# First chunk laid out as two batches by two tokens per partition, W2 loaded by SyncE and cast on chip, and all steps in a new order

## The chip, the cores and the metric

The kernel runs on one core of one Trainium2 chip. The core has five engines that work side by side, each through its own list of instructions, in order: TensorE (PE in the profile; PEld are its weight loads), VectorE (DVE), ScalarE (ACT), GpSimd (POOL) and SyncE (SP), which here only issues DMAs. The metric is the device time of one execution in microseconds; the median of several runs is given. A profile is taken of one execution, and its times count from the first instruction of that execution.

## The reference

The computation has two parts. The first is a linear recurrence over 768 tokens, for 4 batches and 8 heads of width 48:

```
state = 0                                     # per batch and head, 48 x 48
for t in range(768):
    y[t]  = r[t] @ (state + outer(u * k[t], v[t]))
    state = w[:, None] * state + outer(k[t], v[t])
```

`w` (the decay) and `u` have one value per head and channel. The 8 heads of a token, put side by side, make one row of 384 numbers, and the 3072 rows (4 batches by 768 tokens) are the input x of the second part, a feed-forward layer with a squared relu:

```
h   = maximum(x @ w_in, 0)        # 384 -> 2048
out = (h * h) @ w_out             # 2048 -> 384
```

All inputs and the output are 32-bit floats. The kernel multiplies in bf16 and sums in 32 bits.

## The kernel before

**Units.** The tokens are cut into 6 chunks of 128, and a unit is one chunk of one batch: unit i is chunk i // 4 of batch i % 4, 24 in all. Inside a chunk the recurrence is turned into matrix products. k is scaled with powers of the decay that fall with the token's place, r with powers that rise (steps `kh` and `rh`, L336 and L339, into one tile `rk`). `T` (L363) transposes `rk` on TensorE, eight 128 x 128 transposes a unit, and `Tc` copies the result out of PSUM; from unit 7 on a transposing DMA does both (`XB`, L369). `A` (L376) multiplies k by r per head, `Bm` (L384) masks the product to earlier tokens, `Y` (L394) multiplies that with v (in bf16, made by `vb`) and, from the second chunk on, adds r times the state (L392). The term with `u` is computed apart: `P0`, `P1`, `du` and `dv` make the products and sums r*k*u and multiply them into v; `xs` (L411) adds them to Y and gives x. `U` (L403) makes the chunk's contribution to the state, and `S0`, `ts`, `S` keep the state per batch. `X` (L429) and `xTc`, or the DMA `xX`, transpose x.

**Feed-forward.** Units are joined in groups, the first two alone and the others in pairs. `F1` (L445) computes x @ w_in for a group in slices into a PSUM bank, `re` (L453, L455) takes the relu, `sq` (L460 to L464) the square; for a group of two there are 8 slices of 2 x 128 hidden columns. `F2` (L472) sums the product with w_out over the 16 blocks of hidden columns, in quarters of four matmuls per unit; `os` copies the sum out of PSUM, `out` stores it. The last unit is split in two column halves (`F2c`, L486).

**Weights.** w_in is cut into 8 slices `W1[s]`. Seven are loaded in 32 bits by SyncE's queue (`lW`, L324) and cast to bf16 by an engine (`cW`, L260 on ACT or L262 on POOL). One, and all of w_out (`W2`, four slices), are loaded by GpSimd's queue (`W`, L333), which casts on the way.

**Dummies.** `Z` (L498, L500) are matmuls of the identity with itself; their results are not used. They stand at the start, where TensorE has nothing else.

**Order.** There is no scheduler at run time. `ORDER`, a list of steps written out by hand or by a planner ahead of time, sets the list of every engine: `kh.1:D/0` is step kh of unit 1 on DVE into buffer 0. A is ACT, D is DVE, G is GpSimd, P is TensorE, S is SyncE. An engine waits at an instruction until its operands are there and its buffer is free, and everything behind it waits too; that holds for the loads in SyncE's list as well. Buffers per kind are given by `POOLS`; before the change the eight PSUM banks are split into 4 for attention, 2 for F1 and 2 for F2. A DMA that is issued when earlier ones are under way can have to wait at its issuing engine for one of them to end.

Of the kernel before, what the change touches and what calls it, by code (L numbers as in the profile page):

```python
# [19 lines left out]
ORDER = """  # L20
w:A Z.8.4:P Z.8.5:P Z.8.4:P Z.8.5:P Z.8.4:P Z.8.5:P ld.k.1:S/0 ld.r.1:S/0 u:S shw:D shu:D tab:A ld.r.3:S/1 logw:A
Z.6.4:P P0.1:G/0 ld.r.0:S/2 ld.k.0:S/1 Wk:A/0 Wt:A/1 kh.1:D/0 ld.v.1:S/0 rh.3:D/1 ld.k.3:S/2 P1.1:G rh.0:D/2 Z.8.5:P
P0.0:G/1 rh.1:D T.1:P/0 Z.8.4:P Z.5.5:P kh.0:D Tc.1:A/0 Z.6.4:P T.0:P/1 ld.r.2:S/3 Tc.0:A/1 A.0:P/2/3 vb.1:A/0 P0.3:G/2
du.1:D/0 dv.1:G ld.v.0:S/1 A.1:P/0/1 Z.8.5:P Z.8.4:P P1.0:D ld.k.2:S/3 kh.3:D du.0:D/1 Bm.0.1:D/0 P0.2:G/3 P1.3:D
Bm.1.1:D/1 rh.2:D/3 kh.2:D lW.0.1:S/0 T.3:P/3 Tc.3:A/2 lW.0.6:S/1 Bm.0.0:D/2 ld.v.2:S/2 WtS:A cW.0.1:A P1.2:G lW.0.7:S/2
T.2:P/1 Z.8.5:P Z.8.4:P Z.6.5:P Bm.1.0:D/3 lW.0.0:S/3 cW.0.7:G ld.v.3:S/3 Tc.2:A/3 du.2:D/2 Y.1:P/3 vb.0:A/1 xs.1:D/0
A.2:P/2/0 cW.0.6:A vb.2:D/2 dv.0:G X.1:P/1 Y.0:P/3 lW.0.5:S/0 xTc.1:A/0 Bm.2.0:D/4 Bm.2.1:D/5 lW.0.4:S/2 dv.2:G
A.3:P/1/2 wc:S Z.4.4:P Bm.3.0:D/3 cW.0.0:A W.0.2:G xs.0:D/1 du.3:D/3 vb.3:G/3 lW.0.3:S/1 U.2:P/0 F1.1.3:P/1 Bm.3.1:D/1
Y.2:P/1 xs.2:D/2 re.1.3:A/0 X.0:P/3 F1.1.0:P/0 xTc.0:A/1 F1.0.0:P/1 dv.3:G Y.3:P/2 xs.3:D/3 X.2:P/1 ld.r.4:S/4 U.0:P/3
re.1.0:A/1 xTc.2:A/0 W.1.0:G F1.0.3:P/0 cW.0.5:G W.1.1:G X.3:P/2 cW.0.4:A xTc.3:A sq.1.0:A0/0 re.0.0:D/2 ld.k.4:S/4  # L30
ld.r.5:S/5 U.3:P/1 F1.0.2:P/1 WLcol:A re.0.3:D/3 ld.k.5:S/5 re.0.2:D/4 F1.1.2:P/0 sq.0.0:A0/1 W.1.2:G W.1.3:G ld.k.7:S/6
# [530 lines left out]
```

## Time and profile before

| what | value |
|---|---|
| median of 3 runs | 174.29 us (173.12 to 174.57) |
| span of the profiled execution | 172.5 us (the page gives no other time of it) |
| PE, PEld busy | 161.6 us, 121.2 us |
| DVE, ACT, POOL busy | 130.3, 111.1, 80.8 us |
| first F1 on PE | 19.11 us |
| first F1 of units 4 and 5 | 47.72 us |
| last matmuls (F2c) | 166.51 to 169.31 us |
| granted TensorE clock | 1.00 in all stretches |
| DMA | 105588 packets, 98008 of them under 512 B; 29.13 MB |

A row of a timeline gives start, length, engine, line, operation, output and inputs, and the count of instructions merged into it; in brackets stands the idle time ahead of it and what ended that. A row of the groups ends with the total busy time, the mean of one in nanoseconds, and the idle time ahead. A row of the stretches gives for each engine the busy time and the number of instructions, then granted clock, mean busy share of the 16 DMA engines and GB/s moved. In the chain of waits a row is start, length, and what the end of the program was waiting for at that time; SPq is SyncE's queue.

### The profile page before, as it was taken

How to read it: one execution, taken by the hardware profiler on the slowest of the kernel's cores; microseconds unless marked ns; L12 is line 12 of the kernel's file. 1: busy time of each engine (PE TensorE's matmuls, PEld its weight loads, DVE VectorE, ACT ScalarE, POOL GpSimd, SP SyncE). 2: the span in 40 equal slices, each digit the busy share in tenths (PEclk: the TensorE clock that was granted, in tenths of full speed). 3: DMA queues.
4: the chain of work that ended last, by engine and by line, in shares of the span. 5: the costliest groups of instructions: out<-in, count | busy, mean ns of one | idle time of the engine just before them, and what ended most of it. 6: DMA issues, size and time to landing. Idle time of an engine off the chain costs nothing.

```text
span 172.5 us, 4388 instructions
## 1 busy us (share of the span) xinstructions
PE 161.6 (94%) x1702; PEld 121.2 (70%) x1702; DVE 130.3 (76%) x259; ACT 111.1 (64%) x207; POOL 80.8 (47%) x98
## 2 busy tenths in 40 slices
PE   3976799979999999999999999999999999999992
PEld 1444788745788787787778768777778778777671
DVE  5768977739999896598789889888889894538300
ACT  2358787746379899858649647848858726532430
POOL 5644895108659298966937364047660204000000
PEclk9999999999999999999999999999999999999999
DMA  5999899989999989979999997998988330331022
GB/s 99 223 244 306 227 188 207 195 166 200 204 212 184 202 177 214 241 174 184 204 189 215 177 229 153 180 181 186 154 217 159 85 114 4 87 141 48 23 78 84
DMA packets 105588, 29.13 MB, mean 169 GB/s; under 512 B 98008, under 2 KB 105568, under 8 KB 105568
## 3 DMA queue, kind: packets, MB, share of 16 engines
q1 hardware_dynamic: 103672, 26.95, 72.7%
q0 software_dynamic: 1744, 1.77, 6.1%
q8 instruction: 13, 0.21, 0.5%
q10 hardware_dynamic: 152, 0.14, 0.2%
q14 instruction: 7, 0.06, 0.1%
HBM read 20.46 MB, written 4.72 MB: 146 GB/s over the span
## 4 chain that ended last, share of the span: by engine, by line
PE 76%; DMA 12%; SPq 8%; ACT 1%; POOL 1%; issue 1%; DVE 0%; POOLq 0%
PE bank L472 33%; PE bank L445 31%; DMA ldk<-in_k_dram 8%; SPq L320 6%; DMA wsa<-in_moe_w_in_dram 4%; PE bank L376 3%; PE bank L394 2%; PE bank L392 2%; SPq L324 2%; PE bank L403 2%; PE bank L486 2%; PE bank L429 1%; PE bank L363 1%; ACT W L260 1%; POOL urow L218 0%
## 5 line engine op out<-in xcount | busy, mean ns | idle before, releaser
L445 PE MATMUL bank<-xT,W 128*128 128x256 bf16 (+1 forms) x624 | 74.9, 264 | 0.2
L472 PE MATMUL bank<-W,hq 128*128 128x384 bf16 x368 | 69.3, 326 | 0.0
L453 ACT ACTIVATE hr<-bank 128x512 bf16<-128x512 f32 x75 | 44.4, 596 | 32.6 <-PE bank L445 27.1
L445 PEld LDWEIGHTS <-W 128*128 128x128 bf16 x624 | 55.2, 98 | 10.6 <-DVE hr L455 0.3
L472 PEld LDWEIGHTS <-hq 128*128 128x128 bf16 x368 | 34.8, 98 | 17.6
L460 ACT ACTIVATE hq<-hr 128x512 bf16<-128x512 bf16 x65 | 39.1, 628 | 0.3
L384 DVE TENSOR_TENSOR Bm<-bank,maskJT 128x512 bf16<-128x512 f32 x48 | 31.3, 684 | 7.3 <-PE bank L376 7.2
L346 POOL TENSOR_TENSOR P<-P,ub 128x384 f32<-128x384 f32 x15 | 16.1, 1079 | 13.9 <-DVE P L342 13.6
L455 DVE TENSOR_SCALAR hr<-bank 128x512 bf16<-128x512 f32 x21 | 14.3, 687 | 8.5 <-ACT hq L460 3.8
L342 POOL TENSOR_TENSOR P<-ldr,ldk 128x384 f32<-128x384 f32 x14 | 14.3, 1022 | 9.6 <-DMA ldk<-in_k_dram 6.0
L336 POOL TENSOR_TENSOR rk<-ldk,Wkhat 128x384 bf16<-128x384 f32 x10 | 10.0, 996 | 16.9 <-DMA ldk<-in_k_dram 16.9
L411 DVE TENSOR_TENSOR xs<-bank,dv 128x384 bf16<-128x384 f32 x24 | 13.0, 552 | 5.0 <-POOL dv L354 2.8
L354 POOL TENSOR_TENSOR dv<-ldv,du 128x384 f32<-128x384 f32 x18 | 14.8, 829 | 0.0
L349 DVE TENSOR_REDUCE du<-P 128x8 f32<-128x384 f32 x24 | 13.0, 544 | 0.6 <-POOL P L346 0.4
L260 ACT COPY rkT<-bank 128x1024 bf16<-128x1024 bf16 x7 | 7.1, 1012 | 9.1 <-PE bank L363 9.1
L339 POOL TENSOR_TENSOR rk<-ldr,Wt 128x384 bf16<-128x384 f32 x9 | 9.0, 996 | 7.0 <-DMA ldr<-in_r_dram 7.0
L260 ACT CAST vb<-ldv 128x384 bf16<-128x384 f32 x19 | 9.6, 511 | 4.1 <-DMA ldv<-in_v_dram 4.1
L498 PE MATMUL bank<-identity 128*128 128x512 bf16 x29 | 9.5, 471 | 2.7 <-POOL identity masks.py:199 2.7
L260 ACT COPY os<-bank 128x384 f32<-128x384 f32 (+1 forms) x15 | 7.0, 469 | 6.8 <-PE bank L472 4.5
L262 DVE COPY os<-bank 128x384 f32<-128x384 f32 (+1 forms) x10 | 5.2, 524 | 7.9 <-PE bank L486 4.3
L394 PE MATMUL bank<-vb,Bm 128*128 128x48 bf16 x192 | 11.0, 183 | 0.0
L464 DVE TENSOR_TENSOR hq<-hr 128x512 bf16<-128x512 bf16 x27 | 10.9, 432 | 0.0
(66 smaller groups left out, 166.5 us busy)
## 6 DMA issues: line engine op xcount, KB each, us to landing
ldk<-in_k_dram SPq DMA_DIRECT2D x24, 192.0 KB, 3.6
ldr<-in_r_dram SPq DMA_DIRECT2D x24, 192.0 KB, 3.6
ldv<-in_v_dram SPq DMA_DIRECT2D x24, 192.0 KB, 4.0
out_dram<-os SPq DMA_DIRECT2D x23, 192.0 KB, 2.3
wsa<-in_moe_w_in_dram SPq DMA_DIRECT2D x7, 384.0 KB, 5.6
W<-in_moe_w_out_dram POOLq DMA_DIRECT2D x4, 384.0 KB, 9.9
rkT<-rk SPq DMA_TRANSPOSE x17, 3.5
W<-in_moe_w_in_dram POOLq DMA_DIRECT2D x1, 192.0 KB, 6.3
```

The costliest lines, as they stand in the source:

```text
L260: e.copy(o, a)
L342: e.tensor_mul(P0b[slot[f"P{i}"]], loaded("r", i), loaded("k", i))
L346: e.tensor_mul(t, t, ub)
L349: e.tensor_reduce(dub[slot[f"dv{i}"]], P0b[slot[f"P{i}"]], axis=mybir.AxisListType.X, op=ALU.add)
L354: e.tensor_mul(dvb[slot[f"dv{i}"]], loaded("v", i), t)
L384: e.tensor_mul(Bmb[slot[f"Bm{i}{h}"]], heads(bank(f"bA{i}{h}"), 128), mask_b)
L394: e.matmul(y[:, hc, D * h : D * (h + 1)], m[h][:, hc, :], vb[:, 2 * hc + h, :], start=(c == 0), stop=True, skip_group_check=True,)
L445: e.matmul(hp[:, fi, :], W1[f // 2][:, c, 128 * (f % 2) : 128 * (f % 2 + 1)], xt[:, c, :], start=(c == 0), stop=(c == CCH - 1), skip_group ...
L453: e.activation(hr, hp, AF.Relu)
L455: e.tensor_scalar_max(hr, hp, 0.0)
L460: e.activation(hq, hr, AF.Square)
L472: e.matmul(bank(f"bO{i}", "bO")[:, 0:d_model], hqb[slot[f"hq{g},{f // m}"]][:, at : at + L], W2[q][:, f % 4, :], start=(f == 0), stop=(f = ...
```

## The change

Five things change.

1. **Layout of the first chunk.** Units 0 to 3 are no longer one batch each. Two batches share a tile: partitions 0 to 63 hold batch 2p, 64 to 127 batch 2p + 1, and each partition holds two neighbouring tokens. Unit 2p holds the even tokens of both batches, unit 2p + 1 the odd ones. A load then takes runs of 384 B instead of 192 B, and each of r, k, v comes for two units in two DMAs of 64 partitions, one per batch (`ldp`), six of them on SyncE's queue and six on ScalarE's. The scaling tables, masks and outputs follow: two tables each for k and r, a mask per parity, and two stores of 64 rows per unit. On TensorE the products of these units become smaller and more: `A` has 16 matmuls of 64 output rows per unit instead of 8, `Y` 32 of 64 rows instead of 8, because the tokens of a batch are now spread over two units, and `U` runs once for two units with 16 matmuls of 64 input rows. `T` and `Tc` treat r and k apart.
2. **Groups.** The first two units form one group, as all others do: 12 groups of two.
3. **w.** The decay is loaded by SyncE into all 128 partitions at once, without the shuffle on DVE.
4. **Weights.** All 16 halves and slices of W1 and W2 come by SyncE's queue in 32 bits and are cast by ACT, DVE or POOL. They share 9 staging tiles with the first chunk's loads. GpSimd issues no DMA any more.
5. **Order.** All steps stand in a new order with new engines for many of them, F2's quarters of a unit can come in any order, and any step can use any of the 8 banks.

```diff
-GROUPS = [1, 1, 2, 2, 2, 2, 2, 2, 2, 2, 2, 2, 2]
-EARLY = 4
-POOLS = dict(ldr=7, ldk=7, ldv=7, ws=0, wsa=4, rk=7, ..., bank=4, bankH=2, bankO=2, ...)
+GROUPS = [2, 2, 2, 2, 2, 2, 2, 2, 2, 2, 2, 2]
+PAIRED = 4
+POOLS = dict(ldr=6, ldk=6, ldv=6, st=9, rk=7, ...)
...
+w:S nat:G ldp.k.0.1:A/0 ldp.r.0.1:A/1 tab:A logw:A Wtp.1:A Wtp.0:A ldp.r.0.0:S/1 ldp.k.0.0:S/0 rh.0:D/0 Z.65.7:P T.r.0:P/0
+Wkp.1:A P0.1:D/0 rh.1:D/0 ldp.r.1.0:S/2 kh.1:D/1 Z.23.7:P T.k.1:P/1 u:S ldp.v.0.0:S/3 ldp.r.1.1:A/2 shu:D P1.1:D rh.3:D/2
...
+cW.0.3:A lW.0.4:S/7 cW.0.4:A ld.k.5:S/0 kh.5:D/4 xTc.1:A/0 rh.5:G/4 X.0:P/4 xTc.0:A/0 T.5:P/7 Tc.5:A/4 ld.k.4:S/1 F1.0.3:P/4
+P0.3:G/2 Bm.3.0:D/0 re.0.3:A/0 P1.3:D Bm.3.1:D/1 F1.0.4:P/3 Y.2:P/1 ld.r.4:S/1 A.5:P/7/4 lW.0.1:S/8 S0.0:D du.3:D/2 cW.0.1:A
...
+    def two(x, b):
+        t = src[x]
+        return bass.AP(tensor=t.tensor, offset=t.offset + b * H * S * D,
+                       ap=[[2 * D, L // 2], [S * D, H], [1, 2 * D]])
...
+        def ldp(e, x, p, b):
+            e.dma_start(out=staged(f"{x}P{p}").rearrange("p (h x) -> p h x", h=H)[rows[b]], in_=two(x, 2 * p + b))
...
         def lW(e, a, s):
-            t = wsb[("wsa", "ws")[a]][slot[f"ws{a}{s}"]]
-            e.dma_start(out=rows2(t, s) if a else t, in_=weights(a, s))
+            t = staged(f"ws{a}{s}")
+            if a == 0:
+                e.dma_start(out=t.rearrange("p (c n) -> p c n", c=CCH), in_=w_in_t[:, :, 256 * s : 256 * (s + 1)])
+            else:
+                e.dma_start(out=t, in_=w_out_p[s])
...
-        def W(e, a, s):
-            e.dma_start(out=rows2(W2[s], s) if a else W1[s], in_=weights(a, s))
...
         def A(e, i):
+            if i < PAIRED:
+                tk, tr = [rkTb[slot[f"rkT{x}P{i // 2}"]].rearrange("q (j c) t -> q j c t", j=2) for x in "kr"]
+                for hc in range(HP):
+                    for h in range(2):
+                        q = slice(64 * h, 64 * h + D)
+                        for p in rows:
+                            e.matmul(heads(bank(f"bA{i}{h}"), 128)[p, hc, :].rearrange("p (j t) -> p j t", j=2),
+                                     tk[q, i % 2, hc, p], tr[q, :, hc, p], ...)
+                return
...
         def Y(e, i):
+            if i < PAIRED:
+                both = [i - i % 2, i - i % 2 + 1]
+                at = slice(64 * (i % 2), 64 * (i % 2) + 64)
+                for z in both:
+                    for hc, h in [(hc, h) for hc in range(HP) for h in range(2)]:
+                        for p in rows:
+                            e.matmul(y[p, hc, D * h : D * (h + 1)], Bmb[slot[f"Bm{z}{h}"]][p, hc, at],
+                                     vbb[slot[f"vb{z}"]][p, 2 * hc + h, :], ...)
+                return
...
         def U(e, i):
+            if isinstance(i, str):
+                n = int(i[1:])
+                for j in range(2):
+                    for hc in range(HP):
+                        for b, p in enumerate(rows):
+                            e.matmul(heads(bank(f"bU{2 * n + b}"), 2 * D)[:, hc, :], pair(rk[slot[f"rkkP{n}"]][p], j, hc),
+                                     vbb[slot[f"vb{2 * n + j}"]][p, 2 * hc : 2 * hc + 2, :]..., ...)
+                return
...
-        def F2(e, i, q):
+        def F2(e, i, f0, nf):
```

More of the change, by code (lines that the diff above doesn't have):

```diff
@@ L22 @@
[L22 to L31, printed above, removed]
```

403 lines of the change are left out of this document (243 added, 160 removed).

## The prediction

> **What bounds the kernel now.** I read the page first (busy shares, slices), then the same shares by stretch.
>
> ```profile
> span 172.5 us, 4388 instructions
> PE 161.6 (94%) x1702; PEld 121.2 (70%) x1702; DVE 130.3 (76%) x259; ACT 111.1 (64%) x207; POOL 80.8 (47%) x98
> ...
> 0.00:19.10 19.10, 13.36 (x123) 7.43 (x124) 14.12 (x38) 10.13 (x14) 10.17 (x21) 1.00 0.95 223
> 19.10:40.00 20.90, 18.97 (x236) 15.43 (x234) 14.36 (x29) 14.53 (x27) 10.36 (x15) 1.00 1.02 190
> 40.00:166.50 126.50, 126.50 (x1317) 95.96 (x1316) 101.50 (x193) 85.61 (x165) 60.23 (x64) 1.00 0.77 162
> 166.50:172.50 6.00, 2.82 (x34) 2.36 (x31) 0.29 (x1) 0.85 (x2) 0.00 (x0) 1.00 0.19 66
> ```
>
> The columns of the last four rows are PE, PEld, DVE, ACT, POOL busy, granted clock, DMA share, GB/s. From 40 to 166.5 us PE is busy without a gap at clock 1.00: TensorE is the bound there, and no load, cast or drain can be worth anything in that stretch unless it starts to starve PE. The change can win only ahead of 40 us, where PE waits or turns dummy matmuls, and in the last 6 us. So I ask one thing: when does PE reach the same amount of finished work?
>
> ```profile
> 2.70 5.18 PE L498 MATMUL bank<-identity 128*128 128x512 bf16 x13 [2.70 <-POOL identity masks.py:199]
> ...
> 19.11 0.83 PE L445 MATMUL bank<-xT,W 128*128 128x128 bf16 x12
> ...
> 39.12 0.62 PE L363 MATMUL bank<-identity,rk 128*128 128x128 bf16 x8 [1.41 <-DVE rk L336]
> ...
> 47.72 0.66 PE bank L445 x6
> 48.38 0.65 PE bank L472 x4
> ...
> 22.10 2.44 SPq L320
> 24.58 13.90 DMA ldk<-in_k_dram
> ```
>
> The first three rows are PE's timeline, the others the chain of waits. F1 (L445) starts at 19.11; before it there is hardly more than dummies. At 39.12 PE has just lost 1.41 us, because one k load took 13.90 us from 24.58 on. At 47.72 the first F1 of units 4 and 5 starts. That moment is my yardstick: by then F1 and F2 of units 0 to 3 are done but for one F2 quarter.
>
> **The change, part by part.** *The yardstick in the new order.* The same point is F1.2.0. Four F2 quarters of units 0 to 3 come after it, against one before, and T.6 too. A quarter is 0.65 (the row at 48.38) and a T 0.45 (next fence), so F1.2.0 may start at 47.72 - 3 x 0.65 - 0.45 = 45.3 us and be level.
>
> *PE work from the first F1 to F1.2.0.*
>
> ```profile
> 47.27 0.45 PE bank L363 x8
> 45.64 0.34 PE bank L429 x6
> ...
> 11.45 0.62 PE L376 MATMUL bank<-rkT 48*128 48x128 bf16 x16 [1.10 <-ACT rkT L260]
> ...
> 16.28 0.36 PE L394 MATMUL bank<-vb,Bm 128*128 128x48 bf16 x8
> ...
> 18.94 0.33 PE L403 MATMUL bank<-vb,rk 128*128 128x96 bf16 x4
> ...
> L376 PE MATMUL bank<-rkT 48*128 48x128 bf16 x192 | 7.8, 217 | 1.7 <-ACT rkT L260 1.3 <-ACT xT L260 0.5
> L394 PE MATMUL bank<-vb,Bm 128*128 128x48 bf16 x192 | 11.0, 183 | 0.0
> L403 PE MATMUL bank<-vb,rk 128*128 128x96 bf16 x80 | 6.3, 206 | 0.0
> ```
>
> Ends are modelled, so I take a run less its last matmul, divided by the rest: A (0.62 - 0.217)/15 = 27 ns, Y (0.36 - 0.183)/7 = 25 ns, U (0.33 - 0.206)/3 = 41 ns apart. F1 16 x 0.66 = 10.6; F2 12 x 0.65 = 7.8; T.4 0.45; A.4, A.5 16 x 27 ns = 0.4; X.2 to X.5 4 x 0.17 = 0.7; Y.4, Y.5 24 matmuls at 25 to 45 ns, 1.0; U.5 0.2. Y.2 and Y.3 are in the new form, 32 matmuls each in place of 8, of half the rows and half the columns. No row shows such a matmul. Below, it cannot cost less than half of 25 ns (two at once), 0.4 us per unit; above, the 55 ns of an undivided 128-column transpose, 0.45/8, 1.8 us. I take the nearest row, 25 ns: 0.8 each, 1.6. Sum 22.8 us. The column count of F1 is the same (96 matmuls of 128 become 48 of 256), so grouping by two saves PE nothing. The dummies are unchanged: 29 wide, 7 narrow.
>
> *The new small matmuls as a whole.* A, Y and U of units 0 to 3 are 64 + 128 + 32 matmuls instead of 32 + 32 + 16. At 25 to 27 ns that is 5.7 against 2.3 us, nearly all ahead of the first F1 where PE waits anyway. The Trainium skill, TensorEngine Tiling (Array Packing), speaks against this form: under Key Properties a change of tiling mode drains TensorE, and under Restrictions column tiling switches fast weight load off. No run here shows either yet; by it the upper 55 ns would be the likelier one, which is the first rival.
>
> *Start of F1.*
>
> ```profile
> 5.55 0.55 DVE L336 TENSOR_TENSOR rk<-ldk,bank 128x384 bf16<-128x384 f32 x1
> ...
> 6.82 1.02 DVE L339 TENSOR_TENSOR rk<-ldr,bank 128x384 bf16<-128x384 f32 x2 [0.21 <-DMA ldr<-in_r_dram]
> ...
> 12.01 1.04 PE L498 MATMUL bank<-identity 128*128 128x512 bf16 x4
> ...
> 14.49 1.28 DVE L384 TENSOR_TENSOR Bm<-bank,maskJT 128x512 bf16<-128x512 f32 x2
> ...
> 15.74 1.01 ACT L260 COPY rkT<-bank 128x1024 bf16<-128x1024 bf16 x1
> 16.64 0.52 ACT L260 CAST vb<-ldv 128x384 bf16<-128x384 f32 x1
> 17.05 0.89 ACT L260 CAST W<-wsa 128x768 bf16<-128x768 f32 x1
> 17.85 0.48 ACT L260 COPY xT<-bank 128x384 bf16<-128x384 bf16 x1
> ```
>
> The first scaling ran at 5.55. Now w arrives spread over all partitions, without the shuffle, but behind it come two exps instead of one for r; I leave 5.5. DVE then has, in its written order to xs.0, thirteen elementwise steps at 0.51 (1.02/2), two copies or shuffles at 0.5 and six Bm at 0.64: 11.5 us. It also waits about 1 us for T.k.0, which PE holds behind 23 wide dummies from about 2 us on: 13 in 5.2 us (the row at 2.70), ten at 0.2 ((1.04 - 0.47)/3), and two T of half size, so 9.9. xs.0 ends near 18.0. ACT's list is longer. Its first copies wait for DVE's Tc.k.0 (about 10.4) and end near 11.9; then, by starts in the fence, three halves of rkT 1.3 (0.90 for a whole one, from 15.74 to 16.64), four vb 1.6, two W casts 1.6, two xT 0.8, two exps 1.0, wcol 0.4, one DMA issue 0.5: 7.2 us, 19.1; with hand-offs **F1.0.3 at 19.5**. Then both units of the first group are ready, where before had one at 19.11. ACT's DMA issues sit in front of compute: each can wait for an earlier transfer to end, and Wkp.0, kh.0 and T.k.0 are queued behind them. That is 0 to 1 us, taken as 0.3 of the waits below.
>
> *DMA.* Loads of the first chunk move half the packets, of 384 B instead of 192.
>
> ```profile
> 5.00:10.00 5.00, 5.00 (x33) 2.52 (x31) 4.70 (x11) 2.03 (x3) 3.53 (x4) 1.00 1.11 220
> 15.00:17.50 2.50, 2.17 (x31) 1.31 (x29) 1.98 (x6) 2.50 (x5) 0.00 (x0) 1.00 1.10 341
> 24.00:40.00 16.00, 14.44 (x151) 11.25 (x151) 10.60 (x22) 10.62 (x21) 5.46 (x9) 1.00 1.12 189
> ```
>
> While only 192 B loads ran, DMA moved 220 GB/s; with w_in in it (1 KB runs) 341; while POOL's casting loads of W2 ran, 189 (bytes written, half of what they read). Bounds for 384 B are 220 and 341; I take 280. F1.2.0 and what precedes it need first chunk 2.4, w 0.2, W1 and W2 6.3, then eight loads 1.6 MB: 2.4/0.28 + 6.5/0.341 + 1.6/0.22 = 35 us of DMA from about 2 us on. Landing takes another, so the last W2 piece is in at 38 to 40. Used at 41, it holds by 1 to 3 us; at 250 GB/s overall (10.5 MB, 42 us) it would be 4 us late. SP's queue carries 16 weight loads instead of 7, many waiting for a staging slot (lW.0.5 for cW.0.3, lW.1.3 for cW.0.5); loads of units 6 to 9 wait behind them. POOL loses five casting issues and their slow stretch.
>
> *Casts and engines.*
> ```profile
> L453 ACT ACTIVATE hr<-bank 128x512 bf16<-128x512 f32 x75 | 44.4, 596 | 32.6 <-PE bank L445 27.1 <-DVE Bm L384 3.8 <-ACT os L260 0.7
> L460 ACT ACTIVATE hq<-hr 128x512 bf16<-128x512 bf16 x65 | 39.1, 628 | 0.3
> L455 DVE TENSOR_SCALAR hr<-bank 128x512 bf16<-128x512 f32 x21 | 14.3, 687 | 8.5 <-ACT hq L460 3.8 <-PE bank L445 3.3 <-ACT hr L453 1.1
> L464 DVE TENSOR_TENSOR hq<-hr 128x512 bf16<-128x512 bf16 x27 | 10.9, 432 | 0.0
> ```
>
> Eight W2 halves and W1's slice 2 are now cast on chip: nine at 0.9, shared by three engines. Instructions start about 0.1 us before the one ahead is recorded as ended (0.89 us of cast, next start after 0.80), so I subtract 0.08. ACT from xTc.1 to cW.1.2 has 3 xT, 2 rkT, 11 relus, 12 squares and 5 casts: 1.2 + 1.8 + 5.7 + 6.6 + 4.0 = 19.3 us from 18.5, 37.8; the first matmul that needs cW.1.2 stands at 19.5 + 21.5 = 41. DVE from xs.1 to xTc.4 has 46: 6 Bm 3.8, 5 relus 3.0, 4 squares 1.4, 31 others at 0.5, 23.7 us from 16.5, 40.2; F1.2.0 needs it at 42.3. Both lists are covered, by 2 to 3 us, and if that cover goes the wait falls on PE in full. POOL takes 16 r scalings instead of 9 but loses 5 issues and 6 v products; its first F1 weights (cW.0.2, 0.7, 0.5) stand behind twelve steps of about 1.0, near 21 to 23 us, and PE asks for them at 24 to 26. I add 1.0 us of waits for lists this full: F1.2.0 at 19.5 + 22.8 + 1.0 = 43.3, **2.0 us ahead** of 45.3.
>
> *After it* the operations are the same, only reordered (17 transposing DMAs of rk, 10 of xs, 14 X in both). DVE carries 36 relus instead of 21 and 12 v products instead of 6, ACT 60 and 59 relus and squares instead of 75 and 65: DVE goes from 101.5 of 126.5 us to some 110. Four more half-size outs go through SP's queue, each waiting there for its drain with the loads behind it. DMA works at 0.77 there. I count nothing for all this; its cover is the 16 us that DVE still has, and if some list stalls, PE pays directly.
>
> *The end.*
>
> ```profile
> 166.51 2.80 PE L486 MATMUL bank<-W,hq 128*128 128x128 bf16 x32
> ...
> 169.35 0.37 ACT L260 COPY os<-bank 128x256 f32<-128x256 f32 x1 [2.16 <-PE bank L486]
> ...
> out_dram<-os ACTq DMA_DIRECT2D x1, 128.0 KB, 1.7
> out_dram<-os SPq DMA_DIRECT2D x1, 64.0 KB, 1.5
> ```
>
> The last piece out is now the 64 KB one instead of the 128 KB: 0.2 us less.
>
> Span 172.5 - 2.0 - 0.2 = 170.3. The page gives no time around the span; the span lies 1.8 below the median of the runs (174.29; 173.12 to 174.57), and I carry that over: 172.1.
>
> **The rivals.**
> (1) *Small matmuls do not overlap.* About 160 of the 224 lie on the path (A.0 to A.2, U, Y.1 ahead of F1, Y.2, Y.3 in it). Each 10 ns above 25 costs 1.6 us; from 39 ns the gain is gone, at 55 ns it is 172.1 + 4.8 = **176.9**. For: an undivided transpose needs 55. Against: A already runs row halves at 27.
> (2) *DVE or late loads bind.* From F2.0.12.4 to F2.3.4.4 DVE's list is 4 Bm, 3 relus, 5 squares and 24 others, 18.4 us; PE's 13 F2 quarters, 7 F1 and small ones, 15.7. If the 2.7 us shows, or W2 lands 2 us late, the gain goes: **174.3**. For: k took 13.90 us once. Against: the list before was as full there, and PE lost only 1.41.
> (3) *The loads get no faster.* At 220 GB/s for 384 B the first chunk ends 2.4/0.22 - 2.4/0.28 = 2.3 us later, half of it hidden: **173.4**. The Trainium skill, DMA: Bandwidth & Descriptors, Specifications, puts line rate at 512 B and more, which would leave 384 B on the slow side. No run here shows that size.
> (4) *No waits*, and F1 a microsecond sooner: **170.1**.
>
> **How the numbers follow.** Forecast with (3), 171 to 174, 0.47; (4) 0.13; (2) 0.22; (1) and anything over 176 0.18. A measurement of this kernel tells 1%, 1.74 us, from no change: faster means under 172.55. That takes (4) and about 0.35 of the forecast's 0.47: 0.48. Slower is (1) and 0.03 of (2), 0.21; the rest, 0.31, is the same. The range runs from (4) less its spread, 169.2, to just past (1), 177.2.
>
> **What will show it.** First F1 at 18.5 to 20.5; F1.2.0, the first F1 of units 4 and 5, at 42.3 to 44.3; DMA above 250 GB/s over 15 to 30 us; Y.2 at 25 to 30 ns a matmul; no gap in PE after 45. I am wrong if F1 starts after 21.5, if Y's matmuls stand over 40 ns apart, or if PE has gaps between 45 and 160 that add to over 2 us.

## The result, and the profile after

The changed kernel takes 189.28 us (median of 4 runs, 188.75 to 190.27), the kernel before, in the same session, 173.72 (173.12 to 174.57). The ratio is 1.088, with a 95% interval of 1.083 to 1.094: the change makes the kernel 9% slower, where I had forecast 172.1 us. The profiled execution spans 188.6 us against 172.5, 16.1 more.

The page of the changed kernel: span, busy shares, and the engines on the chain that ended last.

```profile
span 188.6 us, 4605 instructions
PE 171.0 (91%) x1798; PEld 123.6 (66%) x1798; DVE 158.0 (84%) x284; ACT 98.3 (52%) x181; POOL 96.7 (51%) x114
...
PE 42%; DVE 32%; DMA 6%; issue 4%; SPq 2%; ACT 1%; DVEq 0%
```

PE had 76% of the chain before; now DVE holds a third of it. Next, PE's timeline of the changed kernel (start, length, engine, line, operation, count).

```profile
27.61 2.76 PE L536 MATMUL bank<-xT,W 128*128 128x256 bf16 x12
30.30 0.69 PE L459 MATMUL bank<-vb,Bm 64*64 64x48 bf16 x32
52.77 0.82 PE L536 MATMUL bank<-xT,W 128*128 128x256 bf16 x6
```

The first F1 starts at 27.61 where I had 19.5, and F1.2.0, the yardstick, at 52.77 where I had 43.3 and where 45.3 would have been level. So 7.5 of the 16.1 us are lost ahead of it, and the other 8.6 behind it. The stretches of both kernels show that: start and end, length, busy time of PE, PEld, DVE, ACT and POOL with instructions in brackets, granted clock, DMA share, GB/s. First the kernel before, from its level point to the end and over 60 to 160 us:

```profile
45.30:172.50 127.20, 124.02 (x1289) 94.92 (x1286) 96.58 (x184) 83.63 (x162) 55.00 (x58) 1.00 0.73 156
60.00:160.00 100.00, 100.00 (x1046) 76.61 (x1041) 80.90 (x154) 67.49 (x131) 46.98 (x49) 1.00 0.76 161
```

The changed kernel, its start, then the same two:

```profile
5.00:10.00 5.00, 4.16 (x20) 1.77 (x19) 1.25 (x3) 2.66 (x5) 0.61 (x1) 1.00 1.34 185
...
15.00:20.00 5.00, 3.84 (x67) 2.31 (x65) 2.87 (x5) 3.76 (x10) 3.10 (x5) 0.84 1.30 160
25.00:30.00 5.00, 4.20 (x31) 3.05 (x30) 4.90 (x11) 3.73 (x6) 2.28 (x2) 0.50 0.98 253
52.77:188.60 135.83, 127.96 (x1286) 94.47 (x1283) 118.35 (x208) 66.21 (x124) 68.76 (x69) 1.00 0.72 144
60.00:160.00 100.00, 95.17 (x985) 69.14 (x984) 94.92 (x162) 53.50 (x101) 64.43 (x65) 1.00 0.84 162
```

Behind the yardstick there are 135.8 us where the kernel before needed 127.2 for the same work. Of the 8.6 us between them 4.7 are idle time of PE (7.9 against 3.2 us); for the other 3.9 PE counts as busy (127.96 against 124.02 us for as many matmuls), and as the ends of matmuls are modelled, the profile does not say what they are. Over 60 to 160 PE idles 4.8 us (before: none) and DVE is busy for 95 of 100 us (before: 81). At the start, over 5 to 20 us, DMA moves 160 to 188 GB/s at a share above 1.2: its engines are busy, but slow. The granted clock is below 1.00 from 10 us on, 0.83 on average over 10 to 25 us and 0.50 over 25 to 30, which the kernel before does not have.

DVE's timeline of the changed kernel ahead of the first F1, and one row of ACT's (in brackets the idle time ahead of a row and what ended it):

```profile
8.18 0.56 DVE L374 TENSOR_TENSOR rk<-st,WtP 128x384 bf16<-128x384 f32 x1 [5.02 <-DMA st<-in_r_dram]
...
9.79 1.35 DVE L374 TENSOR_TENSOR rk<-st,WtP 128x384 bf16<-128x384 f32 x1
11.06 1.34 DVE L368 TENSOR_TENSOR rk<-st,WkP 128x384 bf16<-128x384 f32 x1
...
18.15 1.20 DVE L391 TENSOR_TENSOR dv<-st,du 128x384 f32<-128x384 f32 x1 [2.13 <-issue]
19.28 3.67 DVE L447 TENSOR_TENSOR Bm<-bank,maskP 128x512 bf16<-128x512 f32 x6
...
23.88 0.93 ACT L267 CAST vb<-st 128x384 bf16<-128x384 f32 x2 [2.73 <-DMA st<-in_v_dram]
```

Four things are to be seen. The first scaling waits until 8.18 for r. Scalings that should take 0.55 us take 1.35. DVE stands 2.1 us in front of `dv.1`, with the six masks `Bm`, which PE needs, queued behind it. And ACT stands 2.7 us, until 23.88, for v of the second pair of units, with the copies `xTc` that F1 needs queued behind it.

Groups of DVE's instructions in the changed kernel (total busy time, mean ns of one):

```profile
L449 DVE TENSOR_TENSOR Bm<-bank,maskJT 128x512 bf16<-128x512 f32 x40 | 26.0, 680 | 1.6 <-PE bank L436 1.5 <-ACT hq L551 0.2
L555 DVE TENSOR_TENSOR hq<-hr 128x512 bf16<-128x512 bf16 x37 | 18.6, 521 | 0.3
L370 DVE TENSOR_TENSOR rk<-ldk,Wkhat 128x384 bf16<-128x384 f32 x12 | 10.0, 834 | 0.0
L383 DVE TENSOR_TENSOR P<-P,ub 128x384 f32<-128x384 f32 x12 | 9.9, 828 | 0.1
```

and the same steps of the kernel before:

```profile
L464 DVE TENSOR_TENSOR hq<-hr 128x512 bf16<-128x512 bf16 x27 | 10.9, 432 | 0.0
L336 DVE TENSOR_TENSOR rk<-ldk,Wkhat 128x384 bf16<-128x384 f32 x10 | 7.0, 698 | 1.1 <-DMA ldk<-in_k_dram 1.0
L346 DVE TENSOR_TENSOR P<-P,ub 128x384 f32<-128x384 f32 x9 | 5.0, 551 | 0.0
```

Steps with both operands in SBUF have become longer; the mask `Bm`, with one operand in PSUM, has not (680 ns; 684 before).

### The profile page after: what moved, and what is told of

Same layout as the page of the kernel before. It is cut to its first block, busy times and chain, and to the rows that moved or that the text cites. A ratio compares the mean times of both kernels' runs of the same rounds, so it can differ in the third digit from the quotient of the medians.

```text
span 188.6 us, 4605 instructions
## 1 busy us (share of the span) xinstructions
PE 171.0 (91%) x1798; PEld 123.6 (66%) x1798; DVE 158.0 (84%) x284; ACT 98.3 (52%) x181; POOL 96.7 (51%) x114
## 4 chain that ended last, share of the span: by engine, by line
PE 42%; DVE 32%; DMA 6%; issue 4%; SPq 2%; ACT 1%; DVEq 0%
PE bank L564 19%; PE bank L536 16%; DVE Bm L449 5%; DVE hr L546 4%; DMA st<-in_moe_w_in_dram 4%; DVE du L386 3%; DVE hq L555 2%; DVE P L383 2%; DVE xs L502 2%; DVE rk L370 2%; DVE rk L376 2%; DVE ts L512 2%; DVE P L379 1%; PE bank L436 1%; DMA ldk<-in_k_dram 1%
## 5 line engine op out<-in xcount | busy, mean ns | idle before, releaser
L536 PE MATMUL bank<-xT,W 128*128 128x256 bf16 x576 | 72.4, 276 | 1.0 <-DVE Bm L449 0.5
L544 ACT ACTIVATE hr<-bank 128x512 bf16<-128x512 f32 x60 | 34.6, 593 | 32.9 <-PE bank L536 30.8
L564 PEld LDWEIGHTS <-hq 128*128 128x128 bf16 x368 | 33.5, 98 | 20.5 <-DVE hq L555 2.0
L551 ACT ACTIVATE hq<-hr 128x512 bf16<-128x512 bf16 x59 | 35.3, 627 | 10.8 <-DVE hr L546 10.2
L546 DVE TENSOR_SCALAR hr<-bank 128x512 bf16<-128x512 f32 x36 | 24.2, 683 | 6.3 <-PE bank L536 5.2
L449 DVE TENSOR_TENSOR Bm<-bank,maskJT 128x512 bf16<-128x512 f32 x40 | 26.0, 680 | 1.6 <-PE bank L436 1.5
L376 POOL TENSOR_TENSOR rk<-ldr,Wt 128x384 bf16<-128x384 f32 x15 | 15.9, 1069 | 8.6 <-DMA ldr<-in_r_dram 3.9
L555 DVE TENSOR_TENSOR hq<-hr 128x512 bf16<-128x512 bf16 x37 | 18.6, 521 | 0.3
L515 POOL TENSOR_TENSOR S0W<-ts,WLm 128x384 bf16<-128x384 f32 x11 | 12.5, 1137 | 8.8 <-DVE ts L512 6.3
L267 ACT COPY rkT<-bank 128x512 bf16<-128x512 bf16 (+1 forms) x10 | 6.8, 716 | 8.3 <-DMA st<-in_r_dram 3.3
L469 PE MATMUL bank<-S0W,rkT 128*128 128x96 bf16 x80 | 9.7, 204 | 0.7 <-DVE Bm L449 0.7
```

The lines of the kernel that those rows point to most:

```text
L376: e.tensor_mul(scaled("r", i), loaded("r", i), Wt2)
L449: e.tensor_mul(o, a, mask_b)
L536: e.matmul(hp[:, fi, :], W1[f // 2][:, c, 128 * (f % 2) : 128 * (f % 2 + 1)], xt[:, c, :], start=(c == 0), stop=(c == CCH - 1), skip_group ...
L544: e.activation(hr, hp, AF.Relu)
L546: e.tensor_scalar_max(hr, hp, 0.0)
L551: e.activation(hq, hr, AF.Square)
```

## The experiments

The theories, by the names used in the expectations. For the start: PORTS, RUNS, QUEUES (why the halves come late), SHARING (DVE beside POOL) and LANDING. For the late part: SHARING, LIST (too many steps on DVE), ORDER (the written order itself), QUEUE (loads and SP), LATE PRODUCTS (waiting for POOL's results). Ratios are against the kernel before on the same chip; the changed kernel has 1.088. "Late part" is the time from F1.2.0 to the end of the span: 135.8 us in the changed kernel, 127.2 in the kernel before at the same work. Nine profiles with the changed kernel's own instructions ahead of the first F1 have it at 27.05 to 28.27, so a microsecond there says nothing.

### The first chunk's loads

**e1**: every other partition.

```diff
-  ... "p (h x) -> p h x", h=H)[rows[b]], in_=two(x, 2 * p + b))
+  ... "p (h x) -> p h x", h=H)[b::2], in_=two(x, 2 * p + b))
```

> Each half load of the first chunk now writes every other partition (rows 0, 2, 4 ... or 1, 3, 5 ...) instead of 64 neighbouring ones; bytes, runs of 384 B and queues stay. The two batches' tokens so land interleaved where the rest of the kernel expects halves: the first two chunks' values are not the reference's. Theory PORTS (64 neighbouring partitions reach only half of the ways into SBUF, and that slows all that is in flight): landings of st from r, k, v fall from 6.4 to 8.2 us to 3.5 to 5, windows 5:20 move over 220 GB/s, first F1 at 20 to 23 instead of 27.6, time 182 to 185. Theory RUNS (384 B pieces are slow in themselves): landings within 0.7 us, first F1 within 1 us, time within 1%. Theory QUEUES (issues on ACT and their waits): the same as RUNS.

**e2**: pieces of 3 KB.

```diff
-  ap=[[2 * D, L // 2], [S * D, H], [1, 2 * D]],
+  ap=[[2 * D * H, L // 2], [2 * D, H], [1, 2 * D]],
```

> The half loads read and write 3 KB in one piece per partition instead of eight pieces of 384 B; same partitions, bytes and queues. The values of the first two chunks are other tokens', not the reference's. RUNS: landings of st from r, k, v fall to 3.5 to 5 us, DMA over 5:20 above 220 GB/s, first F1 at 20 to 23, time 182 to 185. PORTS: still 64 neighbouring partitions, so landings above 5.5 us and first F1 after 25, time above 186. QUEUES: first F1 after 26, time within 1%.

**e3**: `ldp.*:A/*` becomes `ldp.*:S/*` in the order.

> All twelve half loads are issued by SP; ACT issues none of them. QUEUES (ACT's issues wait in front of its compute, and two rings take turns): first F1 at 23 to 25.5, time 184 to 187. PORTS and RUNS: ACT's copies still wait for the data; the halves then come one after another instead of together, first F1 at 27 to 30, time 188 to 192.

The stretches of e1, at the start and to the end:

```profile
5.00:10.00 5.00, 3.92 (x23) 1.76 (x21) 2.23 (x3) 2.97 (x6) 1.59 (x2) 1.00 1.25 274
15.00:20.00 5.00, 3.30 (x81) 2.37 (x80) 4.07 (x8) 4.15 (x11) 1.68 (x3) 1.00 1.20 263
47.61:183.80 136.19, 127.14 (x1286) 94.37 (x1283) 117.79 (x208) 66.17 (x124) 68.13 (x68) 1.00 0.72 143
```

of e2:

```profile
5.00:10.00 5.00, 4.53 (x23) 1.97 (x21) 1.75 (x3) 2.65 (x5) 1.11 (x1) 1.00 1.06 222
```

The DMA issues of the changed kernel (KB each, median us to landing):

```profile
st<-in_v_dram ACTq DMA_DIRECT2D x2, 192.0 KB, 8.2
```

In e1 it is 5.0 for the same loads, in e2 7.4.

And PE's first F1 in e1, e2 and e3, in this order:

```profile
24.28 1.47 PE L536 MATMUL bank<-xT,W 128*128 128x256 bf16 x12
```

```profile
27.03 1.47 PE L536 MATMUL bank<-xT,W 128*128 128x256 bf16 x12
```

```profile
24.14 1.47 PE L536 MATMUL bank<-xT,W 128*128 128x256 bf16 x12
```

e1 has the same pieces on the same queues, and only other partitions: over 5 to 20 us the rate is 263 to 274 GB/s instead of 160 to 188 (ratio 1.063, interval 1.052 to 1.073; span 183.8). Eight times longer pieces into the same partitions help much less (e2: 187 to 222 GB/s; its ratio of 1.077, interval 1.067 to 1.088, is not told apart from 1.088). As to the rate, PORTS holds and RUNS is at most a small part. The Trainium skill, SBUF — State Buffer, Door 1, says that 64 neighbouring partitions reach 8 of the 16 ports into SBUF, and its section "Can I just issue two DMAs to hit both halves?" that two such transfers at once gain only 6%; e1 agrees with the first, and the changed kernel's 160 to 188 GB/s, with both halves in flight on two queues, with the second. e2's first F1 cannot be set against e1's: its clock was 0.50 over 15 to 20 us (e1: 1.00), and its DVE, which reaches `dv.1` at 16.87 instead of 18.15, then stands 1.75 us for PE.

The size that I had expected for e1 was too good: F1 at 24.28, not 20 to 23. And e3, with its halves as they were, brings F1 as far forward (24.14, ratio 1.077). What both take away is DVE's 2.1 us wait in front of `dv.1` and ACT's 2.7 us wait for v. The row of `dv.1` names no cause ("issue"), but in the changed kernel ACT issues v's second half at 10.40 and its median landing is 8.2 us; in e3 SP issues all v halves and they land in time. So QUEUES holds too, at the first F1. Since e1 and e3 remove the same waits, their gains need not add; no run has both. Both also have a clock of 1.00 up to the first F1, where the changed kernel's is lower, and a share of their gain may be that. e3 gives most of it back later (late part 138.0 us), and its time is hardly better, where I had expected 184 to 187. PE idles 7.2 us there over 60 to 160, 4.3 of them until transposing DMAs have landed (1.0 in the changed kernel); why they land later is open.

**e9, e10**: the kernel before, with its first loads in halves, neighbouring or interleaved.

```diff
-  e.dma_start(out=loaded(x, i), in_=single[x][i % B, i // B])
+  for p in (slice(0, L // 2), slice(L // 2, L)) if i < EARLY else [slice(0, L)]:   # e10: slice(0, L, 2), slice(1, L, 2)
+      e.dma_start(out=loaded(x, i)[p], in_=single[x][i % B, i // B][p])
```

> The kernel before, with each of the twelve loads of its first chunk cut into two by neighbouring partitions (0 to 63, 64 to 127), both on SP; runs of 192 B and the output stay. Twelve more issues of some 0.6 us on SP. PORTS: DMA over 5:10 falls from 220 to 130 to 180 GB/s, landings of these loads rise, first F1 at 21 to 24 instead of 19.11, time 1 to 2.5% above before. RUNS (only the 384 B pieces were slow) or QUEUES: the same as the strided twin, within 0.7 us at the first F1.

> The twin of the run before it: the two halves are the even and the odd partitions. As many issues, bytes and runs. PORTS: DMA over 5:10 at 200 to 230 GB/s, first F1 at 19 to 21, at least 1.5 us sooner than in the twin. RUNS or QUEUES: no difference from the twin beyond 0.7 us.

e9, its stretch and its issues of k:

```profile
5.00:10.00 5.00, 4.15 (x17) 1.58 (x14) 2.00 (x5) 0.93 (x2) 2.00 (x2) 1.00 0.65 122
L321 SPq DMA_DIRECT2D ldk<-in_k_dram x8: 609/633/752, 0.8 to 14.5; - x8
```

The twins are alike: 122 and 129 GB/s in that stretch, first F1 at 23.93 and 24.48, ratios 1.032 and 1.037. They don't test the ports, and my expectation for them was wrong: an issue of 96 KB holds SP for 633 ns, which is some 155 GB/s at most, so the issue bound the rate and DMA was idle for a third of the time. PORTS is thus shown only where more than one half is in flight. What the twins do show is that a first F1 4.8 and 5.4 us later cost the kernel before 3 to 4%.

### DVE beside POOL in the first chunk

In the kernel before, the early decay weights lie in PSUM; the change put them into SBUF (`WkP`, `WtP`), which I had not weighed. **e5** is e1 with these four in PSUM and POOL's three scalings on DVE; **e15** the same with the loads as they are; **e11** is the kernel before with its two early weights in SBUF.

```diff
-  e.activation(WkP[j], logw, AF.Exp, scale=cols[0][:, j : j + 1])
+  e.activation(banks[5 + j][:, 0 : H * D].rearrange("p (h d) -> p h d", h=H), logw, AF.Exp, ...)
...
- kh.0:G/1 ... rh.2:G/2 ... kh.3:G/3
+ kh.0:D/1 ... kh.3:D/3 rh.2:D/2
```

> On top of the every-other-partition loads: the four decay weights of the first chunk are written by ACT into four PSUM banks, as the kernel before had them, instead of SBUF, and POOL's three scalings of the first chunk (kh.0, kh.3, rh.2) go to DVE. The first two chunks' values are not the reference's, for the reason of e1. Theory SHARING (a DVE step that reads two operands in SBUF takes 1.34 us beside a POOL step instead of 0.55, and holds POOL up too): r and k scalings on DVE at 0.51 to 0.58 us each, first F1 at 20.5 to 22.5 instead of 24.28, F1.2.0 1 to 3 us sooner than 47.61, span 181 to 183 instead of 183.8. Rival LANDING (v's loads and ACT's list set the first F1): first F1 within 0.7 us of 24.3, span within 0.7 of 183.8.

> The kernel before, with the two early decay weights in SBUF instead of PSUM; nothing else. SHARING: the eight early r and k scalings on DVE go from 0.55 to 0.7 to 1.0 us on average (1.3 each where a POOL product runs), POOL's products beside them from 1.00 to 1.2 to 1.35; first F1 0.3 to 2 us later than 19.11, time within 1.5% of before. If SHARING is false: 0.55 us as before, first F1 within 0.2.

> The changed kernel with the loads as they are, the early decay weights in PSUM and POOL's three scalings of the first chunk on DVE; its output is the reference's. SHARING on the path of the first F1: first F1 at 25.5 to 27 instead of 27.61, time 0.5 to 2 us less than the changed kernel's. LANDING (with halves this slow, data sets the first F1): within 0.5 us of both.

The timeline of e1, where DVE and POOL run side by side:

```profile
8.41 1.33 POOL L368 TENSOR_TENSOR rk<-st,WkP 128x384 bf16<-128x384 f32 x1 [3.76 <-DMA st<-in_k_dram]
8.80 1.35 DVE L374 TENSOR_TENSOR rk<-st,WtP 128x384 bf16<-128x384 f32 x1
9.71 1.30 POOL L379 TENSOR_TENSOR P<-st,st 128x384 f32<-128x384 f32 x1
10.08 1.34 DVE L368 TENSOR_TENSOR rk<-st,WkP 128x384 bf16<-128x384 f32 x1
```

and of e5, at the same place:

```profile
8.44 1.34 POOL L382 TENSOR_TENSOR P<-st,st 128x384 f32<-128x384 f32 x1 [3.79 <-DMA st<-in_k_dram]
8.85 0.55 DVE L377 TENSOR_TENSOR rk<-st,bank 128x384 bf16<-128x384 f32 x1
9.31 0.55 DVE L371 TENSOR_TENSOR rk<-st,bank 128x384 bf16<-128x384 f32 x1
...
23.46 1.47 PE L539 MATMUL bank<-xT,W 128*128 128x256 bf16 x12
```

The groups of e11:

```profile
L337 DVE TENSOR_TENSOR rk<-ldk,early_WkP 128x384 bf16<-128x384 f32 x4 | 3.8, 957 | 0.1
```

A scaling with one operand in PSUM takes 0.55 us beside a POOL product, with both in SBUF 1.35; POOL's product takes 1.30 to 1.34 instead of 1.00. (e5's POOL row is long because the product r*k on DVE, with both operands in SBUF, is at work from 8.37 to 8.93.) e11 makes the same change in the kernel before: 0.957 us for k and 0.795 for r instead of the 0.55 quoted in the prediction. SHARING holds as a price per step. The Trainium skill, SBUF — State Buffer, Who interferes with whom, says that a DVE instruction with two SBUF inputs contends with a GpSimd instruction that reads SBUF, and with one SBUF input does not; that is what e1 and e5 show. By the page the second to issue is blocked until the first ends, and the rows of e1 agree: they end at 9.74 (POOL), 10.15 (DVE), 11.01 (POOL) and 11.42 (DVE), so a DVE step ends 0.41 us after POOL's and a POOL step 0.86 after DVE's. The two take turns. A long row is a wait followed by a step of about the usual length (e5's scalings start 0.46 us apart), and while both have such steps they get done one after the other.

On the path no gain is clear. e5 has its first F1 0.8 us ahead of e1 (23.46, not the 20.5 to 22.5 expected), with three steps more on DVE, but F1.2.0 no sooner (47.88 against 47.61), and its ratio of 1.057 (interval 1.047 to 1.067) is not told apart from e1's; e18 below, with the same steps up to there, has its first F1 at 25.05. e15, with the slow halves, gains nothing: first F1 at 28.61, a microsecond later than in the changed kernel, and the ratio again 1.088. `dv.1`, which needs v, starts at 18.23 there (18.15 in the changed kernel), so up to that step LANDING holds; behind it DVE stands 1.7 us for PE, whose clock was 0.50 over 20 to 25 us, and this hides what the shorter steps might have brought. e11 has its first F1 2.9 us later (22.01; at most 2 expected) and yet the same time (1.003, interval 0.999 to 1.007): the kernel before had slack there. Its 1.4 us wait for k at 39 us, ahead of the yardstick, is gone from the trace of e11.

### W2

**e8** lets POOL's casting loads bring W2 again.

```diff
- ... all of lW.1.*:S/* and cW.1.*
+ W.2:G cW.0.2:G W.3:G ... cW.0.6:G W.0:G W.1:G
```

> W2 comes by POOL's casting loads again (four of them, issued between the casts of W1 on POOL): 8 loads less on SP's queue, 8 casts less (ACT 3, DVE 1, POOL 4, by the written order). If the W2 part of the change costs (queue and casts in front of later steps): F1.2.0 at 49 to 51 instead of 52.77, time 184 to 187. If it is covered, as I had it: F1.2.0 within 1 us of 52.8 and time within 1% of 189.3. If the casting loads are the dearer way: time above 191.

Its F1.2.0 is at 54.45, 1.7 us later than in the changed kernel, and its ratio 1.095 (1.086 to 1.104) is not below 1.088. So W2 on SP's queue with casts on chip costs no more than POOL's casting loads, and is not where the time went.

### The late part

**e4** moves the relus `re.2` to `re.10` from DVE to ACT (`:D/` becomes `:A/`). **e6** and **e7** leave steps out when the order is read, **e12** both:

```diff
+        if eng[0] == "G" and name in ("P0", "P1", "dv", "rh", "kh", "S") and at[-1] >= 8:   # e6, e12
+            continue
+        if eng[0] == "D" and name in ("P0", "P1", "du", "dv") and at[-1] >= 6:              # e7, e12
+            continue
         getattr(Do, name)(E[eng[0]], *at, *map(int, eng[1:]))
```

> The 26 relus that DVE has in groups 2 to 10 go to ACT; nothing else changes. Theory DVE (from 60 us on DVE's list is the bound): DVE's busy time falls by 26 x 0.69 = 17.9 us to 140, PE's idle time over 60:160 falls from 4.8 us to under 1.5, time 183 to 186. Rival ORDER or LATE DATA (PE waits for work that is late for other reasons, DVE only happens to be full): PE's idle time over 60:160 stays above 3.5, time within 1% of 189.3. A third way: ACT becomes the bound in its place, ACT busy above 18.5 us of each 20, time 188 or more.

> POOL's 57 products of units 8 to 23 (P0, P1, dv, rh, kh, S) are left out; readers use old data, so those units' values are not the reference's. DVE's, ACT's and PE's instructions stay. SHARING: DVE's two-operand steps in SBUF fall from 0.83 to 0.55 to 0.6 us (rk L370, P1 L383), DVE busy from 158 to 140 to 148 us, PE idle over 60:160 from 4.8 to under 2 us, time 179 to 184. Rival LIST (DVE simply has too many steps, whatever POOL does): means within 5%, DVE busy above 155, time above 186. Rival ORDER (PE's order and the drains set the pace): DVE's means may fall, but PE's idle time stays above 3.5 us and the time above 186.

> DVE's 38 steps P0, P1, du, dv of units 6 to 23 are left out (old data is used, so those units' values are not the reference's); POOL keeps all of its steps. DVE's busy time falls by 38 x 0.55 to 0.83, some 24 us, to 134. If DVE is the bound from 60 us on (SHARING and LIST): PE idle over 60:160 under 2 us, time 179 to 184. ORDER: PE idle above 3.5, time above 186.

> The changed kernel without POOL's 57 products of units 8 to 23 and without DVE's 38 steps P0, P1, du, dv of units 6 to 23 (old data is used; those units' values are not the reference's). If what is left of the late loss is DVE's list (LIST): PE idle over 60:160 under 1 us, span 178 to 181. If it is the written order with its transposing DMAs (ORDER): PE still waits for rkT and xT from DMA, idle above 2 us, span 182 to 184.

The stretches of e6, the late part and 60 to 160 us, and then of e7:

```profile
52.55:183.10 130.55, 125.00 (x1285) 94.75 (x1283) 105.04 (x208) 66.33 (x124) 8.79 (x11) 1.00 0.74 149
60.00:160.00 100.00, 97.40 (x1045) 73.63 (x1043) 86.97 (x172) 53.52 (x101) 5.85 (x8) 1.00 0.84 164
```

```profile
60.00:160.00 100.00, 95.47 (x1005) 71.16 (x1003) 75.99 (x130) 52.62 (x100) 60.53 (x63) 0.98 0.85 161
```

Groups of e6:

```profile
L555 DVE TENSOR_TENSOR hq<-hr 128x512 bf16<-128x512 bf16 x37 | 15.2, 428 | 1.3 <-ACT hr L544 1.0
L370 DVE TENSOR_TENSOR rk<-ldk,Wkhat 128x384 bf16<-128x384 f32 x12 | 7.0, 585 | 0.3 <-DMA ldk<-in_k_dram 0.3
L383 DVE TENSOR_TENSOR P<-P,ub 128x384 f32<-128x384 f32 x12 | 6.6, 550 | 0.1
```

Moving 26 relus off DVE brings nothing: PE's idle time is 5.7 us (4.8 in the changed kernel), the ratio 1.096. But 4.1 of the 5.7 us now end on ACT, which got the relus, so e4 trades one list for another and says little about LIST. e7 says more: with 38 DVE steps left out DVE is busy for 76 of 100 us, less than in the kernel before, and yet PE still idles 4.5, the late part is 134.7, the ratio 1.079 (interval 1.072 to 1.087). So LIST, the long list on DVE taken alone, falls. What PE waits for in e7 is mostly no longer DVE but the transposing DMAs of rk (waits of PE: total, times, longest):

```profile
PE bank L436 <- DMA rkT<-rk: 3.7, 4, 1.2
PE bank L536 <- DVE Bm L449: 0.7, 1, 0.7
```

Without POOL's 57 products (e6) the late part is 130.6 (ratio 1.065) and DVE's steps are back at 550, 585 and 428 ns. PE idles 2.6 us, not the under 2 that I had expected, and all of it ends on DMA, 1.3 us on `xT<-xs` and 1.3 on `rkT<-rk`, the transposes. Leaving out both (e12) is no better than POOL's alone: 132.4 us, and the ratio 1.069. My expectation of under 1 us idle for LIST failed, and the 1.9 us by which its late part is longer than e6's stay unexplained.

**e13** leaves out the loads of units 8 to 23 once their slot has been filled, **e14** these and POOL's products. **e16** and **e17** (with loads, and without) keep POOL's products, but send them where nobody reads. **e18** is e5 and e14 together.

```diff
+        if name == "ld":                                         # e13, e14, e17, e18
+            key = (at[0], slot[f"{at[0]}{at[1]}"])
+            if at[1] >= 8 and key in filled:
+                continue
+            filled.add(key)
...
-  e.tensor_mul(P0b[slot[f"P{i}"]], loaded("r", i), loaded("k", i))
+  e.tensor_mul(WtP[0] if e is nc.gpsimd and i >= 8 else P0b[slot[f"P{i}"]], ...)   # e16, e17; so for P1, dv, rh, kh, S
```

> The changed kernel without the loads of r, k, v of units 8 to 23 wherever their slot has been filled once (old data is used; those units' values are not the reference's). POOL and DVE keep their steps, SP keeps transposing DMAs and outs. Theory QUEUE (SP's queue and the DMA engines, full from 5 to 130 us, bring rk and its transposes late): DMA share over 60:140 from 0.9 to 1.06 to under 0.6, PE idle over 60:160 from 4.8 to under 2.5 us, span 182 to 186. SHARING plus ORDER: PE idle stays above 4, span within 1 us of 188.6.

> The same without POOL's 57 products of units 8 to 23 as well. QUEUE and SHARING together: PE idle over 60:160 under 0.7 us, span 179 to 181.5, against 183.1 with POOL's products alone left out. ORDER: PE idle as there, 2.6 us, span within 0.7 of 183.1.

> The changed kernel; POOL's 57 products of units 8 to 23 run as before on the same inputs, but write to a spare buffer; readers use old data and never wait for POOL (values of those units are not the reference's). SHARING (POOL's work slows DVE's two-operand steps): DVE's means stay at 0.75 to 0.85 us (rk L370, P1 L383), DVE busy above 153, PE idle over 60:160 above 3.5, span 186.5 to 189. Rival LATE PRODUCTS (readers wait for POOL): as with the products left out, PE idle about 2.6 us and span 182.5 to 184.5.

> The same without the loads of units 8 to 23 wherever their slot has been filled once. SHARING: like e13, PE idle above 3, span 185 to 187.5. LATE PRODUCTS: like e14, PE idle under 0.7, span 178 to 181.

> Everything found taken away at once: every-other-partition loads, early decay weights in PSUM, no POOL products of units 8 to 23, no loads of units 8 to 23 into filled slots (values not the reference's). If the causes account for the whole: first F1 at 23 to 24, F1.2.0 at 45.5 to 48, PE idle over 60:160 under 0.7 us, 127 to 128 us from F1.2.0 to the end, span 173 to 176. If something is missing: more than 129 us behind F1.2.0.

The stretches of e14, e16, e17 and e18, in this order:

```profile
51.34:178.80 127.46, 124.58 (x1285) 94.81 (x1283) 104.73 (x208) 66.17 (x124) 8.86 (x11) 1.00 0.39 88
60.00:160.00 100.00, 100.00 (x1070) 76.08 (x1066) 89.06 (x176) 55.72 (x106) 5.92 (x8) 1.00 0.39 83
```

```profile
52.90:189.00 136.10, 127.54 (x1285) 94.31 (x1283) 117.46 (x207) 66.31 (x124) 68.62 (x68) 1.00 0.71 141
```

```profile
53.60:188.30 134.70, 127.45 (x1286) 94.72 (x1283) 116.70 (x208) 66.26 (x124) 68.48 (x68) 1.00 0.39 84
```

```profile
49.47:176.90 127.43, 124.57 (x1286) 94.84 (x1283) 104.02 (x207) 66.18 (x124) 9.02 (x11) 1.00 0.37 84
```

The largest of PE's waits in e13:

```profile
PE bank L436 <- DVE xs L502: 0.9, 2, 0.6
PE bank L469 <- DVE Bm L449: 0.8, 1, 0.8
```

Without loads alone the late part is 134.0 us and the time does not change (e13, ratio 1.086). Without loads and POOL's products it is 127.5 us with PE busy for all of the 100 (e14, ratio 1.048): the whole late loss is gone, 5.3 us with POOL's products and 3.1 more with the loads. When POOL works but nobody waits for it (e16), the late part is 136.1 (ratio 1.097), as if nothing were changed: LATE PRODUCTS alone falls. e17 is the sharpest of these runs. It differs from e14 only in that POOL's products run, and nobody reads them; the late part is 134.7 instead of 127.5 us, and PE's waits of 0.2 us and more, 3.9 in all, end on DVE without exception (its steps are at 790, 806 and 519 ns there). So POOL's work by itself, through the turns that DVE has to leave to it, costs these 7 us.

The waits of all these runs sort into two kinds. Those for DVE are gone or small where POOL's products (e6, e14) or DVE's 38 steps (e7) are left out, or both (e12). Those for transposing DMAs are gone where the loads are left out (e13, e14, e17). Only where both are gone does PE not idle (e14, e18); where one goes, the other stays or grows, so their prices don't add up. What delays the transposes in e7 is open: SP's queue, where the loads stand too, is one candidate, POOL's late rk another (SP stood 3.6 us in front of them for POOL's rk and 3.1 for DVE's). A short DVE list without loads, with POOL's results awaited, would decide it and was not run.

ORDER stays untested in one sense. The kernel before has POOL busy for 55.0 us of its late part, against 68.8, and its PE does not idle over 60 to 160 us. The runs show what removes the loss, but none gives back the old division of the steps or the old order, so how much is due to which of the two is not shown.

e18 takes all these away at once: late part 127.4, as expected, ratio 1.022 (interval 1.012 to 1.032). Its first F1 at 25.05 and its yardstick at 49.47 are later than the 23 to 24 and 45.5 to 48 that I expected, and 1.6 us later than in e5 with the same steps ahead of them. Its clock was 0.67 over 15 to 20 us (e5: 1.00), and DVE stood 1.76 us for PE there. Up to there the two runs have no other difference, so the clock is the likely cause, and gains of a microsecond or so at the start, as of e5 over e1, are not certain. No version of the changed kernel that does all of its work comes near the kernel before.

## Why the prediction was wrong

The forecast span of 170.3 became 188.6: 9.5 us were added ahead of F1.2.0 (43.3 became 52.77), and 8.8 behind it (127.0 became 135.8). The 47.72 of the kernel before was read from the chain of waits; its timeline has this F1 at 47.56, so the level point is 45.1 to 45.3.

- **"Start of F1": "The first scaling ran at 5.55 ... I leave 5.5."** Failed, by 2.7 us (8.18). The weights alone allowed no start before 6.70: ACT had w at 5.02 (4.38 in the kernel before), and the table that `rh.0` reads is the second of two exps, 6.10 to 6.70. After that the step still waited for r. At most 0.5 us of this is the slow rate: e1 and e3 still start at 7.63 and 7.68. A unit now holds rows of two batches, so its first step needs two DMAs of 192 KB where before it needed one; I had moved the loads without asking how many a first step waits for. That this is the rest of the wait was not tried alone.
- **"Thirteen elementwise steps at 0.51."** Failed. The row priced was `rk<-ldr,bank`, with a PSUM operand; in the new kernel it is `rk<-st,WtP`, beside a POOL product, at 1.35. Of the thirteen, two scalings took 1.35 and 1.34, a third 0.80, and the two `dv` 1.20 and 1.36; the others were near their price. The price was in the name of the operand. With the weights and the rate repaired (e5) the sum comes out: 23.46 is 19.5 plus 2.15 of later start, three extra steps at 0.55, and 0.2. Part of that is luck, as e18 reached 25.05 with the same steps.
- **"xs.0 ends near 18.0", ACT's list at 19.1.** Failed, with the two above and the waits for v: xs.0 ended at 25.81, and ACT, held up for v until 23.88, came to the copies `xTc` at 26.28. F1 followed at 27.61.
- **"DMA": 384 B pieces between 220 and 341 GB/s, 280 taken.** Missed, at 160 to 188, and below my lower bound, so rival (3) was too mild. For the piece size the number was fair: e1 moves 384 B pieces at 263 to 274. The partitions that the halves write were not in the sum at all.
- **"ACT's DMA issues ... 0 to 1 us, taken as 0.3."** That issues on ACT can come late was right, the size and the place were wrong: v's second half, issued by ACT at 10.40, held DVE for 2.1 us with `Bm` behind it, and the second pair's v held ACT for 2.7. SP alone (e3) or quicker halves (e1) put the first F1 3.5 and 3.3 us ahead.
- **PE work from the first F1 to F1.2.0, 22.8 us and 1.0 of waits.** 25.2 measured, 1.4 more than 23.8. The clock accounts for 1.3: the first twelve matmuls took 2.76 us at a granted clock of 0.50, against 1.47 in e1. **Y at 25 ns**: 32 matmuls in 0.69 us, under 22 ns each. Rival (1) is dead; what the Trainium skill, TensorEngine Tiling (Array Packing), has against such matmuls under Key Properties and Restrictions shows no cost in these rows.
- **W2 and its casts covered**: right as far as e8 can tell.
- **"After it ... I count nothing; its cover is the 16 us that DVE still has."** Failed, by 8.6 us, nearly half of the miss. DVE did not go to 110 of 126.5 us but to 118.35 of 135.8: I had added its new steps at the old means, and beside a busier POOL they are not the old ones (521 against 432 ns for the squares, 828 against 551 for P1), since DVE has to wait its turn (e17 against e14). The sentence that "if some list stalls, PE pays directly" was the right one, and the cover the wrong one: PE stood idle where DVE was busy for 76 of 100 us (e7). The transposes, late behind loads, were a second wait that the sum put at nothing (3.1 us, e6 against e14).
- **The end, 0.2 us less**: PE's last matmul ends 3.0 us from the end (182.75 + 2.80 = 185.55 of 188.6), against 3.2 before. Right.
- **Chances.** Rival (2), DVE or late loads, named the two things that PE waits for in the late part, but put them ahead of F1.2.0, counted DVE's steps at their old length, and priced the whole at 2 us; behind F1.2.0 it was 8.6, in many stalls. That it named the right two is partly luck. Rival (3) comes to 173.3 by its own terms, not 173.4. The range held nothing slower than 177.2, for no rival joined two causes.

## What to carry to other kernels

Price an elementwise step by where its operands lie and by what runs beside it, not by its operation: a step whose operand moves from PSUM to SBUF went from 0.55 to 1.35 us beside POOL here, because the two then took turns. When a load is cut by partitions, ask how many ports its rows reach and how many DMAs the first consumer then waits for. Free time on an engine is no cover for a new order: see what stands in front of each step that TensorE waits for. And before two starts are compared, look at the granted clock of both.
